# Moving the copies of keys and queries into block rows from the middle of a down stage to behind its output stores (mLSTM cell followed by a GELU layer)

## The chip, the cores and the metric

The kernel runs on one core of a Trainium2 chip. The metric is the device time of one execution in microseconds. A profile of one further execution gives the span from its first to its last instruction and what each engine did: TensorE (PE, with its weight loads PEld), VectorE (DVE), ScalarE (ACT), GpSimd (POOL) and SyncE (SP), which here does nothing but issue DMA transfers, one after the other.

## The reference

Two layers, one behind the other. The first is a recurrent cell over 4 batches, 8 heads, 768 steps and a head size of 40; its result, reshaped to 3072 rows of 320, goes through a feed-forward layer of width 2048 with an exact GELU.

```python
for t in range(S):
    m_new = np.maximum(f_gate[:, :, t] + m, i_gate[:, :, t])
    f_stab = np.exp(f_gate[:, :, t] + m - m_new)
    i_stab = np.exp(i_gate[:, :, t] - m_new)
    m = m_new
    C = f_stab[..., None, None] * C + i_stab[..., None, None] * einsum('bhd,bhe->bhde', vt, kt)
    n = f_stab[..., None] * n + i_stab[..., None] * kt
    y[:, :, t] = sigmoid(o_gate[:, :, t]) * einsum('bhde,bhe->bhd', C, qt) / max(|n.qt|, 1)
x = y.transpose(0, 2, 1, 3).reshape(3072, 320)
out = gelu_exact(x @ w_in) @ w_out
```

## The kernel before

The 768 steps are cut into six chunks of 128 (`c` = 0 to 5). For each chunk and each of the four batches `b` the cell is computed in its parallel form: masked decay weights `W` (loaded from `M_d`, masked on POOL, exponentiated on ACT), scores from `kT` and `qT`, values, and an update of the carried `state`. The 512 rows of a chunk then go through the feed-forward layer: an **up stage** (`up`, line 926: products with `w_in`, GELU into `g`) and a **down stage** (`down_steps`, line 1052: products of `g` with `w_out` into `po`, added up in `o_sb` and stored to `out`). PE runs them in turn: up of chunk 1, down of chunk 1, up of chunk 2, and so on. The cell of chunk `c + 1` is woven into the two stages of chunk `c`. The order within a down stage is written out by hand in the string `DOWN` (line 36), which `play` (line 1115) follows letter by letter: `F` is the next of 14 steps of down products, `M`, `W`, `G`, `S`, `C`, `V`, `Y`, `X`, `R` and others are steps of the cell, and `j` is `load_next`. Every engine executes its instructions in the order in which they were written.

From chunk 2 on, keys and queries are not transposed on PE. They are first copied from their input arrays into a scratch array in device memory, `kq_d`, in an order of block rows (`copy_chunk`, line 156: for each batch two DMAs of keys and two of queries, 80 KB each, 16 in all for a chunk). Later `load_blocks` (line 164, four DMAs) reads one batch of them into the tile `blocks` (or `blocks3` for the last batch), and DVE transposes that tile in 32 by 32 squares into `kT` and `qT` (`turn_k`, `turn_q`).

All these transfers stand in one queue, SP's, in the order written. In the built program each DMA of that queue also waits, ahead of being issued, for the one eight places before it to have landed. Around the change the queue holds, for a stage `c`:

- in the down stage: the block rows of batch 3 (`load_last`), the decay weights of batch 3 into a part of `g` (`last_M`), keys and values of batch 3; then at `j` the block rows of batch 0 of chunk `c + 2`, followed by `copy_chunk(c + 3)`;
- at the end of the down stage: the stores of `o_sb`. The twelfth `F` ends the product whose follow-up is `p3` (line 1099): a DVE addition into `o_sb[0]` and four stores (`send`, line 1025, two for each of two batches). The fourteenth and last `F` ends the one with `p4` (line 1104), likewise with four stores. The letters behind `j` are `R0 Y2 Y3 X1 F F X2 R1 F R2 X3 R3 F`;
- in the up stage of chunk `c + 1`: behind the transposes of batch 0 the block rows of batch 1 (`turn_q`), then the `later_loads` (line 979): weights `W`, keys `kb`, values `vb` and gates `ob` of the next cell, and behind the transposes of batch 1 the block rows of batch 2.

`copy_chunk` is called in four places of the kernel: for part of chunk 2 in the first part of the program, for the rest of chunk 2 and for chunk 3 in the up stage of chunk 1, and in `load_next` for chunk 4 (down stage of chunk 1) and chunk 5 (down stage of chunk 2). In the down stages of chunks 3 and 4 nothing is left to copy. A copied chunk is first read at `j` of the following down stage.

Of the kernel before, what the change touches and what calls it, by code (L numbers as in the profile page):

```python
# [41 lines left out]
def kernel(  # L42
# [18 lines left out]
    B, H, S, D = q.shape  # L61
    L = P
    NCH = S // L
# [92 lines left out]
    def copy_chunk(c, batches=range(B)):  # L156

        for b in batches:
            for i, src in enumerate((k, q)):
                for hip in range(2):  # L160
                    nc.sync.dma_start(out=kq_d[c - 2][b, hip].rearrange("(m i x t) d -> i x m (t d)", m=NP, i=2, x=16)[i],
                                      in_=src[b, hip::2, c * L:(c + 1) * L, :].rearrange("m (x t) d -> x m (t d)", x=16))

    def load_blocks(n, to):

        c, b = divmod(n, B)
        for hip in range(2):
            for d, w in ((0, 32), (32, D - 32)):
                nc.sync.dma_start(out=to[64 * hip + d:64 * hip + d + 32].rearrange("t m i (g w) -> t (m i g) w", w=32)[:, :, 0:w],
                                  in_=kq_d[c - 2][b, hip, :, d:d + w].rearrange("(x t) d -> t x d", t=32))  # L170
# [254 lines left out]
    class Cell:  # L425
# [73 lines left out]
        def load_next(self):  # L499
            if self.c + 1 < NCH:  # L500
                load_blocks((self.c + 1) * B, by_block)
            if self.c + 2 < NCH:
                copy_chunk(self.c + 2)

        def weigh_last(self, b):
            if self.c < NCH - 1:
# [518 lines left out]
    def send(c, b, o_sb):  # L1025
        to = out[b * S + c * L:b * S + (c + 1) * L, :]
        if c == 0:
            nc.sync.dma_start(out=to, in_=o_sb)
            return
        for a in range(2):  # L1030
            queue = nc.scalar if a and c == NCH - 1 else nc.sync
            queue.dma_start(out=to[halves[a]], in_=o_sb[a::2])
# [19 lines left out]
    def down_steps(c, g):  # L1052
        A = lambda e, h: lambda j, t: g.t[:, HF * e + j, HT * h + t * L:HT * h + (t + 1) * L]
        Sm = lambda s: lambda j, t: s[j // (HF // 2)][:, j % (HF // 2), t * L:(t + 1) * L]
        bank, o_sb = {}, {}

        def product(lhs, rhs, k, first, t, then):

            if first and t == 0:
                bank[k] = ps_mm.tile([P, 2, HD], F32, name="po", tag="b")  # L1060
            for j in range(HF):

                nc.tensor.matmul(bank[k][:, t, :], lhs(j, t), rhs(j), start=(first and t == 0 and j == 0),  # L1063
                                 stop=(t == 1 and j == HF - 1), skip_group_check=True)
            if t == 1:
                then(bank[k])

        def block(h, n):
            if h not in o_sb:
                o_sb[h] = outp.tile([P, 2, DM], F32, name="o_sb", tag="o_sb")  # L1070
            return o_sb[h][:, :, HD * n:HD * (n + 1)]

        def add(to, pb, x):
            nc.vector.tensor_tensor(out=to, in0=pb, in1=x, op=OP.add)


        def p1(pb):
            nc.scalar.copy(out=block(1, 1), in_=pb)

        def p6(pb):  # L1080
            add(block(1, 0), pb, block(1, 1))

        def p2(pb):
            nc.scalar.copy(out=block(0, 0), in_=pb)

        def sum_late():
            for i in range(2):
                a12 = g.t[:, HF + HF // 2 * i:HF + HF // 2 * (i + 1), 0:HT]
                nc.vector.tensor_tensor(out=a12, in0=a12, in1=g.s2[i], op=OP.subtract)

        def p5(pb):
            add(block(1, 1), pb, block(1, 0))

        def p7(pb):
            add(block(1, 1), pb, block(1, 1))
            if c == NCH - 2:
                nc.sync.dma_start(out=w_out[:, 0:HF, HD:], in_=right_d)

        def p3(pb):
            add(block(0, 1), pb, block(1, 0))  # L1100
            for t in range(2):
                send(c, t, o_sb[0][:, t, :])

        def p4(pb):
            add(block(1, 0), pb, block(1, 0))
            for t in range(2):
                send(c, 2 + t, o_sb[1][:, t, :])

        todo = ((A(0, 0), Bm[0][0], 0, True, p1), (Sm(g.s2), T[2], 1, True, p6),
                (A(1, 0), Bm[1][0], 0, False, p2), (Sm(g.s1), T[1], 2, True, p5),  # L1110
                (A(0, 1), T[3], 3, True, p7), (A(1, 0), Bm[1][1], 2, False, p3),
                (A(1, 1), T[4], 3, False, p4))
        return [lambda x=x, t=t: product(*x[0:4], t, x[4]) for x in todo for t in range(2)], sum_late

# [36 lines left out]
    for c in range(1, NCH):  # L1151
        if c + 1 == NCH:
            down = LastDown()
            up(None, [], [], down)
            down.products()
            break
        g, later = Hidden(True), []
        steps = cell_steps(c + 1, "MWGTscVYXRLKQDCBSjh", g)
        up(g, weight_sum(1) + weight_sum(2) + weight_sum(3) if c == 1 else [], [lambda b=b: (steps["K"](b), steps["Q"](b)) for b in range(2)])
        if c == 1:  # L1160
            later = weight_sum(4)
        products, late = down_steps(c, g)
        steps |= dict(F=in_turn(products), Z=in_turn(later), N=late)
        play(DOWN, steps)
# [30 lines left out]
```

## Time and profile before

| what | us |
|---|---|
| median of three runs | 462.73 (462.39 to 462.76) |
| the profiled execution | 462.86 |
| its span, first to last instruction | 460.7 |
| down stage of chunk 1 on PE | 153.82 to 198.35 |
| up stage of chunk 2 | 198.35 to 224.85 |
| down stage of chunk 2 | 224.85 to 268.09 |
| up stage of chunk 3 | 268.09 to 294.59 |
| down stage of chunk 3 | 294.59 to 337.29 |
| issue of the 16 copies of chunk 4 on SP | 174.54 to 188.02 |
| issue of the 16 copies of chunk 5 on SP | 245.14 to 257.98 |
| one copy from issue to landing, median | 2.5 |
| one store of `o_sb` from issue to landing, median | 2.0 |

The stages are read off the chain of work that ended last, where the first products of a stage (`pu` at line 947 for up, `po` at line 1063 for down) begin. A time on SP is the time that the issue of a DMA takes on that queue; the transfer itself runs on 16 DMA engines that all queues of the core share, and lands later. "Idle before" names what an engine waited for; "issue" there means a gap for which the profile shows no releaser.

### The profile page before, as it was taken

What the parts mean: (1) busy time and instruction counts of PE and PEld (TensorE: products, weight loads), DVE (VectorE), ACT (ScalarE), POOL (GpSimd) and SP (SyncE); (2) the same over time, 40 slices, a digit from 0 to 9 for tenths busy, and PEclk for the clock granted to TensorE, in tenths of its full rate; (3) what the DMA queues carried; (4) which work ended last, traced back from release to release, by engine and by line L of the source; (5) the groups of instructions that cost most, each with busy time, mean ns of one, the idle gap of its engine ahead of it and who ended that gap; (6) DMA issues with size and microseconds to landing.
All of it is one profiled execution on the core that took longest, in us unless ns stands there. A gap on an engine that the chain in (4) does not pass through costs nothing.

```text
span 460.7 us, 13113 instructions
## 1 busy us (share of the span) xinstructions
PE 451.9 (98%) x5432; PEld 402.0 (87%) x5432; DVE 308.7 (67%) x661; ACT 243.7 (53%) x541; POOL 76.7 (17%) x117
## 2 busy tenths in 40 slices
PE   9999999999999998999999999999999999999996
PEld 8787888877788898998899998899998899988996
DVE  8677457573579987755578754578654577699950
ACT  7886999953244593113494113395113395257701
POOL 3001030000010432200542200542300422100000
PEclk9999999999999999999999999999999999999999
DMA  7999962295857655219945219853018950200001
GB/s 168 221 221 223 232 177 69 82 242 125 166 129 158 113 96 98 57 51 182 167 79 103 59 57 184 154 92 46 3 57 168 172 94 15 80 35 1 1 0 58
DMA packets 174875, 51.12 MB, mean 111 GB/s; under 512 B 154752, under 2 KB 168352, under 8 KB 174816
## 3 DMA queue, kind: packets, MB, share of 16 engines
q1 hardware_dynamic: 174496, 49.95, 51.0%
q8 instruction: 43, 0.70, 0.6%
q10 hardware_dynamic: 320, 0.33, 0.2%
q14 instruction: 16, 0.13, 0.1%
HBM read 45.47 MB, written 10.03 MB: 120 GB/s over the span
## 4 chain that ended last, share of the span: by engine, by line
PE 95%; DVE 2%; issue 1%; DMA 1%; ACT 1%; SPq 0%; DVEq 0%
PE po L1063 26%; PE pu L947 23%; PE po L1042 8%; PE pu L804 6%; PE pu L958 6%; PE po L917 6%; PE ph L655 4%; PE ps L553 3%; PE pu L810 2%; PE ps L537 2%; PE px L695 2%; PE pf L608 2%; PE pt L515 1%; PE cold L226 1%; PE pf L619 1%; PE pf L575 1%
## 5 line engine op out<-in xcount | busy, mean ns | idle before, releaser
L1063 PE MATMUL po<-w_out,g 128*128 128x160 f32 x512 | 74.4, 302 | 0.0
L962 ACT ACTIVATE g<-pu 128x512 f32<-128x512 f32 x64 | 32.2, 618 | 77.4 <-PE pu L958 77.4
L1063 PEld LDWEIGHTS po<-w_out,g 128*128 128x128 f32 x512 | 70.1, 190 | 1.9 <-ACT g L962 1.3
L947 PE MATMUL pu<-x_hi,w_in_hi 128*128 128x512 f32 x160 | 39.0, 387 | 0.0
L465 ACT ACTIVATE W<-W,aT 128x128 f32<-128x128 f32 x128 | 38.7, 387 | 0.1
L947 PE MATMUL pu<-x_lo,w_in_lo 128*128 128x512 f32 x160 | 37.8, 379 | 0.0
L1063 PE MATMUL po<-w_sums,sums 128*128 128x160 f32 x256 | 36.9, 302 | 0.0
L439 POOL TENSOR_SCALAR_AFFINE_SELECT W<-W 128x1024 f32<-128x1024 f32 (+2 forms) x20 | 24.1, 1209 | 75.8 <-DMA W<-M_d 66.8
L1063 PEld LDWEIGHTS po<-w_sums,sums 128*128 128x128 f32 x256 | 35.0, 190 | 0.4
L1042 PE MATMUL po<-w_out,g 128*128 128x320 f32 x128 | 35.2, 433 | 0.0
L947 PEld LDWEIGHTS pu<-x_hi,w_in_hi 128*128 128x128 f32 x160 | 29.5, 189 | 5.7 <-ACT g L962 1.3
L947 PEld LDWEIGHTS pu<-x_lo,w_in_lo 128*128 128x128 f32 x160 | 30.2, 189 | 4.3
L1042 PEld LDWEIGHTS po<-w_out,g 128*128 128x128 f32 x128 | 24.0, 190 | 9.6
L524 POOL TENSOR_TENSOR vw<-vb,ewT 128x328 f32<-128x328 f32 x12 | 8.7, 737 | 138.5 <-DMA vb<-in_v_dram 55.9
L947 PE MATMUL pu<-x_all,w_mid 128*128 128x512 f32 x80 | 30.3, 379 | 0.0
L947 PE MATMUL pu<-x_all,w_in_mid 128*128 128x512 f32 x80 | 30.3, 379 | 0.0
L559 DVE TENSOR_TENSOR W<-ps,W 128x256 f32<-128x256 f32 (+1 forms) x48 | 18.1, 416 | 17.0 <-PE ps L553 7.1
L804 PE MATMUL pu<-first_x,w_in 128*128 128x256 f32 x128 | 28.8, 381 | 0.0
L804 PEld LDWEIGHTS pu<-first_x,w_in 128*128 128x128 f32 x128 | 23.8, 190 | 3.1
L791 DVE TENSOR_TENSOR sums<-g 128x512 f32<-128x512 f32 x16 | 12.3, 770 | 19.6 <-ACT g L962 19.6
L763 DVE TENSOR_TENSOR w_in_mid<-w_in_hi,w_in_lo 128x512 fp32r<-128x512 f32 x20 | 13.7, 686 | 16.5 <-PE pu L947 16.5
L385 DVE SCALAR_TENSOR_TENSOR pow<-sig,pow 128x320 uint32<-128x320 uint32 (+1 forms) x26 | 14.6, 563 | 13.7 <-ACT pow L375 13.7
(195 smaller groups left out, 917.5 us busy)
## 6 DMA issues: line engine op xcount, KB each, us to landing
W<-M_d SPq DMA_DIRECT2D x16, 512.0 KB, 5.4
bits<-in_moe_w_in_dram SPq DMA_DIRECT2D x20, 256.0 KB, 4.5
bits<-in_moe_w_out_dram SPq DMA_DIRECT2D x16, 320.0 KB, 3.2
blocks<-kq_d SPq DMA_DIRECT2D x32, 128.0 KB, 3.6
ob<-in_o_gate_dram SPq DMA_DIRECT2D x24, 160.0 KB, 3.9
out_dram<-o_sb SPq DMA_DIRECT2D x36, 80.0 KB, 2.0
kq_d<-in_k_dram SPq DMA_DIRECT2D x32, 80.0 KB, 2.5
kq_d<-in_q_dram SPq DMA_DIRECT2D x32, 80.0 KB, 2.5
```

The source lines that it names most:

```text
L385: nc.vector.scalar_tensor_tensor(out=p, in0=s, scalar=3, in1=p, op0=OP.logical_shift_left, op1=OP.bitwise_or)
L439: nc.gpsimd.affine_select(out=x, in_=x, compare_op=OP.is_ge, fill=1.0e30, base=base, pattern=[[0, H], [1, x.shape[2]]], channel_multiplier=-1)
L465: nc.scalar.activation(out=W[n][:, h, :], in_=src, func=AF.Exp, scale=-1.0, bias=aT[:, self.c, r:r + 1])
L559: nc.vector.tensor_tensor(out=w[r, :, t], in0=ps[i][hip][r, :, t], in1=w[r, :, t], op=OP.mult)
L655: nc.tensor.matmul(ph[r, h, :], Pm[:, h, r], vb[turn_of(n)][:, h, :], start=True, stop=True)
L804: nc.tensor.matmul(banks[-1][e][:, i - i0, :], in_tile(i, x)[:, e, i % 2 * P:(i % 2 + 1) * P], first_x[:, x, t0:t1], start=(x == 0 and i = ...
L917: nc.tensor.matmul(in_pairs(po[t]), x[:, t * L:(t + 1) * L], in_turns(w), start=(f, k) == first, stop=(f, k) == last, skip_group_check=True)
L947: nc.tensor.matmul(in_pairs(pus[i][e]), w[k][:, e, i * P:(i + 1) * P], in_turns(x[:, k, :]), start=(n == 0 and k == 0), stop=False, skip_g ...
L958: nc.tensor.matmul(in_pairs(pu[e]), w[r, i // 2, i % 2 * P:(i % 2 + 1) * P], in_turns(x[r, NX, :]), start=False, stop=(n == 2), skip_group ...
L962: nc.scalar.activation(out=g.t[:, HF * e + i, :], in_=pu[e], func=AF.Gelu, scale=4097.0)
L1042: nc.tensor.matmul(po[b], g.t[:, f, b * L:(b + 1) * L], w_out[:, f, :], start=(f == 0), stop=(f == NF - 1))
L1063: nc.tensor.matmul(bank[k][:, t, :], lhs(j, t), rhs(j), start=(first and t == 0 and j == 0), stop=(t == 1 and j == HF - 1), skip_group_che ...
```

## The change

`load_next` no longer calls `copy_chunk`. The 16 copies of chunk `c + 3` are issued by the down stage's own follow-ups instead: those of batches 0 and 1 behind the four stores of `p3`, those of batches 2 and 3 behind the four stores of `p4`. `c` in `load_next` is the chunk of the cell, one more than the chunk of the down stage, so the same chunks 4 and 5 are copied in the down stages of chunks 1 and 2.

```diff
         def load_next(self):
             if self.c + 1 < NCH:
                 load_blocks((self.c + 1) * B, by_block)
-            if self.c + 2 < NCH:
-                copy_chunk(self.c + 2)
@@
             for t in range(2):
                 send(c, t, o_sb[0][:, t, :])
+            if c + 3 < NCH:
+                copy_chunk(c + 3, range(2))
 
         def p4(pb):
             add(block(1, 0), pb, block(1, 0))
             for t in range(2):
                 send(c, 2 + t, o_sb[1][:, t, :])
+            if c + 3 < NCH:
+                copy_chunk(c + 3, range(2, B))
```

On PE, DVE, ACT and POOL the built program has the same instructions with the same waits in the same order; only the order on SP differs, in two places.

## The prediction

> **What bounds the kernel now.** I read the page first, then the time by stage, then SP's queue, then PE's waits.
>
> ```profile
> PE 451.9 (98%) x5432; PEld 402.0 (87%) x5432; DVE 308.7 (67%) x661; ACT 243.7 (53%) x541; POOL 76.7 (17%) x117
> ...
> 153.82:198.35 44.53, 42.87 (x813) 41.28 (x814) 35.84 (x84) 23.79 (x60) 14.89 (x22) 1.00 0.47 88
> 224.85:268.09 43.24, 42.86 (x813) 41.29 (x814) 31.60 (x68) 23.79 (x60) 15.04 (x22) 1.00 0.47 86
> 294.59:337.29 42.70, 42.65 (x813) 41.17 (x814) 30.70 (x68) 23.77 (x60) 16.30 (x21) 1.00 0.37 59
> ```
>
> PE is busy 451.9 of 460.7 us at full granted clock (the 1.00). The lower lines are the down stages of chunks 1, 2 and 3: length, then busy time of PE, PEld, DVE, ACT, POOL. PE is idle in them for 1.66, 0.38 and 0.05 us. All three run the same PE instructions, and only the first two hold copies. So the most a removal of the copies from the middle can bring is small, and the change loses only if PE starts to wait for a transfer.
>
> ```profile
> 193.94 7.36 SPq L1032 DMA_DIRECT2D out_dram<-o_sb  x8
> 206.10 2.29 SPq L169 DMA_DIRECT2D blocks<-kq_d  x4
> ...
> 223.58 6.76 SPq L169 DMA_DIRECT2D blocks<-kq_d  x8
> 231.46 0.38 SPq L186 DMA_DIRECT2D g<-M_d  x1
> 236.82 1.29 SPq L151 DMA_DIRECT2D kb<-in_k_dram  x2
> ...
> 248.66 1.23 SPq L161 DMA_DIRECT2D kq_d<-in_k_dram  x2
> 249.93 1.23 SPq L161 DMA_DIRECT2D kq_d<-in_q_dram  x2
> ```
>
> This is SP's timeline (start, length, what) from the end of the down stage of chunk 1 on. Single rows of it give the stores as 193.94 to 196.42 (`p3`) and 198.91 to 201.30 (`p4`, whose DVE addition starts at 198.39). Then SP waits 4.80 us for the DVE transpose of batch 0, which ends at 206.08. From 206.10 to 230.34 it issues one load after another. The `g` load waits for DVE's sums until 231.46, and the `kb` load for PE until 236.82.
>
> ```profile
> PE pf L619 <- issue: 1.1, 1, 1.1
> PE ph L655 <- issue: 0.3, 1, 0.3
> ```
>
> These are PE's own waits without a releaser: the first at 175.92 to 177.03 in the down stage of chunk 1, the second at 253.26 to 253.59 in that of chunk 2 (0.42 by the weight loads). Both lie where copies are in flight.
>
> **Part 1: what leaves the middle.** Sixteen issues go from SP in each of two stages (174.54 to 188.02, 245.14 to 257.98). The next on SP are the stores, which wait for DVE until 193.94 and 263.68, 5.9 and 5.7 us after the last copy, so the queue gains nothing there. What may gain is PE's instruction supply. The DMA queue marked "instruction" moved 43 packets, 0.70 MB, 16 KB each; that is 256 instructions of 64 B if all are PE's, and 43 x 256 = 11,008 fits PE's 10,864 matmuls and weight loads. In windows of a tenth of a microsecond, such a packet starts at 174.6 (1.10 us long by its share of the 16 engines) and at 251.2 (0.96 us). PE resumes 2.43 and 2.39 us after those starts. I therefore take both gaps as waits for instructions, in bursts of very short matmuls. How much of them the copies cause:
> - Chunk 1: at 174.6 the engines were over 90% busy with the block loads issued from 171.33, which stay; the first copy was only issued at 174.54. Bounds 0 and 1.11 us; I take 0, the row of the block loads being nearer.
> - Chunk 2: the packet itself took 0.96 us, as did those at 317.0 and 323.2 in chunk 3 with no copies (0.97, 0.96), and the wait behind it fell where the engines were idle (252.4 to 253.1). Only the time ahead of the packet can have been lengthened. Bounds 0 and 0.54 us, the whole difference to the stage of chunk 3 (43.24 - 42.70); I take 0.2, about half of the 0.42 gap.
>
> [...]
>
> **Part 2: what the end of the stage takes on.** In the quiet stretch 248.66 to 251.20 four copies took 2.54 us, 0.635 each. Behind the stores of `p3`: 8 x 0.635 = 5.08, 196.46 to 201.54. The stores of `p4`, ready at about 198.9, are pushed to 201.54 to 204.0 (2.6 us later). Nothing needs them soon: their tile is next written by ACT at 229.43. Then eight copies to 209.1. None waits long for the eighth before it, which was issued 5 us earlier and lands in 2.5. So the block rows of batch 1 are issued 3.0 us later (209.1 for 206.10), and the loads behind them, which stood without a gap, likewise. What each is needed for (landing: longest of `blocks` 5.5, median of `g` 4.8):
> - `blocks`, batch 1: landed by 216.9; DVE transposes it at 220.06 as its program order has it.
> - `vb`: POOL waited for it until 221.07, now 224.1. Behind it come a mask of W, a clearing of the block tile that started at 224.75, and the mask of the second W, which ended at 229.45 and will by about 230.7 (the clearing starts some 1.2 later). ACT reaches that W after eight exponentials from 231.17, at 233.6.
> - `blocks`, batches 2 and 3: landed by 238.8; DVE needs them at 240.24.
> - `g`: issued at about 233.8 and landed by 238.6; POOL masks it at 239.30.
> - `kb`: SP is free again at about 234, and it waits for PE until 236.82 anyway.
>
> So the lateness ends there, in SP's own waits. Chunk 1 shows the same lateness already: copies of chunk 3 stood in the queue before its down stage, and its `g` load is issued at 161.69 to 163.41, 9.6 us into the stage, against 7.0 in chunk 2.
>
> ```profile
> 161.69 1.72 SPq L186 DMA_DIRECT2D g<-M_d  x1
> ...
> 168.28 1.81 POOL L439 TENSOR_SCALAR_AFFINE_SELECT g<-g 64x1024 f32<-64x1024 f32 x2
> ...
> 239.30 1.81 POOL L439 TENSOR_SCALAR_AFFINE_SELECT g<-g 64x1024 f32<-64x1024 f32 x2
> ```
>
> The mask came 14.46 us into that stage (168.28 - 153.82) and 14.45 into chunk 2's, so 2.6 us of lateness cost nothing. Cost of this part: 0. If the cover were gone, each further microsecond would cost up to one per stage, twice. Instruction packets at the new place (213 and 231) feed an up stage of 146 matmuls in 26.5 us, where a late packet stalls nothing.
>
> **Sum.** -0.2 + 0 = -0.2 us: 462.66 for the profiled execution, which is 460.7 of span and 2.16 around it. It stands 0.13 above the median, so 462.5 for the median.
>
> **Rivals.**
> 1. Both gaps are the copies' doing and vanish: -(1.11 + 0.54) = -1.65, 461.1. For it: both lie beside copies and the stage without copies has none. Against it: the block loads at 174.6; besides, where the supply runs short depends on where a block of 256 instructions ends in a burst, and that differs from stage to stage.
> 2. The lateness outgrows its cover. In the middle of chunk 1 the first four copies took 174.54 to 178.20, 0.91 each. SP has 2.49 (between the stores) and 4.80 us idle to take them up, so the shift is 16 x 0.91 - 7.3 = 7.3 us. The cover of `g`: SP was done at 230.34 and may be done by 234.4 (239.30 less 4.8, less the issue) for no delay, 4.1; ACT's wait behind the mask (241.11 to 241.75) gives 0.6; and POOL's result of 247.54, which DVE takes at 248.52, 1.0: 5.7 in all. Beyond that PE's transposes of `y` come late: 2 x (7.3 - 5.7) = +3.2, 465.9. It decides from a shift of 5.7 us, 0.81 a copy. For it: the average of the 16 in the middle was 0.80 (12.84 / 16). Against it: those pauses came while block loads kept the engines busy, and at 196 to 206 only the stores run.
> 3. The copies run where they are put and no term above exists: 462.73. It differs from the forecast by less than can be told.
>
> **How the numbers follow.** A difference of 0.2% (0.93 us) is about what a measurement of this kernel can tell from no change. The forecast and rival 3 hold 0.54; rival 1, 0.22; rival 2, 0.24, higher than its rows alone would give, since the chain of loads behind the copies is long and one tight consumer that I passed over suffices. Rivals 1 and 2 lie beyond 0.2%, so faster 0.22, same 0.54, slower 0.24. The range starts at rival 1, less 0.1, and reaches to 464.4, a shift of 6.6 us (+1.7), which leaves out the further part of rival 2 and a little below.
>
> **What would show it.** SP's timeline: the block rows of batch 1 at about 209 and 279 instead of 206.10 and 275.85, the mask of `g` still 14.45 us into the stages of chunks 2 and 3. The down stage of chunk 1 still 44.5 with its gap at 177, that of chunk 2 at 43.0. The forecast is wrong if PE waits for `ps`, `pf` or `px` in the down stages of chunks 2 or 3, or if the gap of chunk 1 is gone.

## The result and the profile after

The changed kernel ran at a median of 463.68 us over 20 runs (462.70 to 465.90), the kernel before beside it at 462.44 (20 runs, 461.85 to 463.56): a ratio of 1.0026 with a 95% interval of 1.0016 to 1.0036. It was slower, by little. The profiled execution was one of the shortest of the 20 (462.74, span 460.6), so its total says nothing of the loss; its stages show where PE lost time. Four later comparisons of the same two kernels, on four chips, gave 1.000 to 1.0013 (experiments 1, 5, 10 and 14), so the loss is not the same everywhere.

The down stages of chunks 1, 2 and 3 after the change (window, length, then busy time of PE, PEld, DVE, ACT, POOL, granted clock, DMA share, GB/s):

```profile
153.57:197.82 44.25, 42.87 (x813) 41.28 (x814) 35.77 (x84) 23.79 (x60) 15.86 (x22) 1.00 0.36 60
224.32:267.47 43.15, 42.87 (x813) 41.29 (x814) 31.73 (x68) 23.81 (x60) 15.01 (x23) 1.00 0.44 72
293.96:337.15 43.19, 42.94 (x814) 41.34 (x814) 31.80 (x68) 23.90 (x60) 16.95 (x23) 1.00 0.46 78
```

Chunk 1 is 0.28 us shorter and chunk 2 0.09, but chunk 3, in whose down stage nothing was ever copied, is 0.49 longer (42.70 before; a second profile of the kernel before, experiment 9, has 43.43, 43.16 and 42.98, so one profile tells differences of this size only roughly). That stage comes right after the up stage whose loads now stand behind the copies of chunk 5. SP's timeline there (start, length, what):

```profile
265.56 1.29 SPq L161 DMA_DIRECT2D kq_d<-in_k_dram  x2
266.89 2.59 SPq L161 DMA_DIRECT2D kq_d<-in_q_dram  x2
...
272.14 2.46 SPq L1030 DMA_DIRECT2D out_dram<-o_sb  x4
...
279.82 2.92 SPq L169 DMA_DIRECT2D blocks<-kq_d  x4
...
297.61 7.27 SPq L169 DMA_DIRECT2D blocks<-kq_d  x8
305.05 0.58 SPq L186 DMA_DIRECT2D g<-M_d  x1
305.94 1.60 SPq L151 DMA_DIRECT2D kb<-in_k_dram  x2
```

The block rows of batch 1 start 12.35 us into the up stage (279.82 - 267.47; 7.76 before, so 4.6 late), and the `g` load 11.1 us into the down stage (305.05 - 293.96) instead of 6.6. In the up stage of chunk 2 the delay is 3.3 (208.84 - 197.82 = 11.02 for 7.75). POOL now waits for `g` (the bracket is the idle time before and its releaser):

```profile
239.39 1.81 POOL L439 TENSOR_SCALAR_AFFINE_SELECT g<-g 64x1024 f32<-64x1024 f32 x2 [0.57 <-DMA g<-M_d]
...
309.84 1.80 POOL L439 TENSOR_SCALAR_AFFINE_SELECT g<-g 64x1024 f32<-64x1024 f32 x2 [1.37 <-DMA g<-M_d]
```

The mask comes 15.07 and 15.88 us into the two stages, for 14.45. PE's own waits, however, still name no engine beyond those of before:

```profile
PE pf L617 <- issue: 0.8, 1, 0.8
...
PE ph L653 <- issue: 0.2, 1, 0.2
PE pf L606 <- issue: 0.2, 1, 0.2
```

The first is still that of chunk 1 (1.1 before), without a copy in that stage's middle. The last is new, and lies in chunk 3.

### The profile page after: what moved, and what is told of

Read it like the earlier page. It is cut to its first block, busy times and chain, and to the rows that moved or that the text cites. A ratio compares the mean times of both kernels' runs of the same rounds, so it can differ in the third digit from the quotient of the medians.

```text
span 460.6 us, 13113 instructions
## 1 busy us (share of the span) xinstructions
PE 452.0 (98%) x5432; PEld 401.5 (87%) x5432; DVE 310.8 (67%) x661; ACT 243.7 (53%) x541; POOL 76.5 (17%) x117
## 4 chain that ended last, share of the span: by engine, by line
PE 92%; DVE 4%; ACT 1%; DMA 1%; issue 1%; SPq 0%; DVEq 0%
PE po L1061 26%; PE pu L945 23%; PE po L1040 8%; PE pu L956 6%; PE po L915 6%; PE pu L802 5%; PE ph L653 4%; PE ps L551 3%; PE ps L535 2%; PE pf L606 2%; PE px L693 2%; PE pu L808 2%; PE pt L513 1%; PE pf L617 1%; PE pf L573 1%
## 5 line engine op out<-in xcount | busy, mean ns | idle before, releaser
L557 DVE TENSOR_TENSOR W<-ps,W 128x256 f32<-128x256 f32 (+1 forms) x48 | 18.1, 416 | 16.7 <-PE ps L551 7.1
L703 ACT ACTIVATE x_hi<-px 128x384 fp32r<-128x384 f32 x20 | 9.7, 486 | 25.6 <-PE px L693 25.6
```

The lines of the kernel that those rows point to most:

```text
L557: nc.vector.tensor_tensor(out=w[r, :, t], in0=ps[i][hip][r, :, t], in1=w[r, :, t], op=OP.mult)
```

## The experiments

Four theories were told apart. Q: SP's loads are pushed back behind the copies. T: the copies' traffic at the border of the stages does it, whatever the queue. Q was later split into M (the late mask of `g` holds up ACT, VectorE and PE) and S (the late `g` load shares the DMA engines with PE's packets of instructions, and PE runs dry). Each had up to 12 timed runs beside the kernel before; diffs are against the changed kernel. "Stages" are the lengths of the down stages of chunks 1, 2 and 3 in the profile, good to about 0.01 us.

**1. The changed kernel again** (no edit).

> The changed kernel itself once more, for a second profile and more times: about 1.0026 of before. Theory Q (the queue): the loads of the up stage stand behind 16 copies on SP and start 3 to 4.5 us later, and the decay weights of batch 3 (g) come too late for POOL, ACT and then PE; a profile of a typical execution (463.2 and more) shows the down stage of chunk 3, chunk 2 or both 0.5 to 1.5 us longer than before (42.70 and 43.24), with POOL waiting for the DMA of g by 0.6 to 3 us. Theory T (the traffic): the copies slow something at the border of the stages by sharing the DMA engines there; then the up stages of chunks 2 and 3 (26.50) or the last products of the down stages before them are longer, and POOL's wait for g does not go with the loss.

Measured: 1.000 (0.9987 to 1.0013). Stages 43.70, 43.15, 42.71. Here `g` is issued 10.2 us into the stage of chunk 3, and that stage loses nothing. The loss is not there in every execution, and this profile shows none of it.

**2. Half of the copies behind p3, half at j.**

```diff
             if self.c + 1 < NCH:
                 load_blocks((self.c + 1) * B, by_block)
+            if self.c + 2 < NCH:
+                copy_chunk(self.c + 2, range(2, B))
...
-            if c + 3 < NCH:
-                copy_chunk(c + 3, range(2, B))
```

> Batches 0 and 1 are copied behind the stores of p3, batches 2 and 3 at j as before. Eight copies take 5.1 us of SP, and it has 2.5 and 4.8 us idle there: the block rows of batch 1 start at most 0.3 us later. Theory Q: 1.000 of before (0.999 to 1.0005), and g masked 14.45 us into the stages of chunks 2 and 3. Theory T: half of the traffic is at the border, so about half of the loss, 1.0013.

Measured: 0.9992 (0.9982 to 1.0002), stages 43.44, 43.15, 43.01. Block rows of batch 1 at 7.75 us, `g` at 6.61, mask at 14.45, all as before. So eight copies do fit into SP's idle time, as theory Q has it. The time does not part Q from T, since the changed kernel itself was at 1.000 on that chip.

**3. The copies behind p4 issued by ACT.**

```diff
-    def copy_chunk(c, batches=range(B)):
+    def copy_chunk(c, batches=range(B), queue=nc.sync):
...
-                copy_chunk(c + 3, range(2, B))
+                copy_chunk(c + 3, range(2, B), nc.scalar)
```

> As the changed kernel, but the eight copies behind the stores of p4 are issued by ACT, which is idle there for 11 us until the GELUs. The same traffic at the same place, but SP's loads are not pushed. Theory Q: the loss is gone, 0.9985 to 1.0003 of before, block rows of batch 1 within 0.5 us of the place they have before. Theory T: the loss stays, about 1.0026.

Measured: 0.999 (0.998 to 1.000), stages 43.20, 42.88, 42.72. SP's loads are where they were, and every stage is among the shortest seen. All 16 copies are still at the border of the stages, but not quite where the changed kernel has them: ACT issues its eight from 2.1 us before the up stage to 3 or 4 us into it, while SP in the changed kernel issues them 6 to 12 us into it. So this run speaks against T without settling it. What settles it are the up stages, in which the copies now run: T expects them longer, and those of chunks 2 and 3 take 26.49 or 26.50 us in every profile, of before and after alike.

**4. Only the copies of chunk 5 moved.**

```diff
+            if self.c + 2 < NCH - 1:
+                copy_chunk(self.c + 2)
...
-            if c + 3 < NCH:
+            if c + 3 == NCH - 1:
                 copy_chunk(c + 3, range(2))
...
-            if c + 3 < NCH:
+            if c + 3 == NCH - 1:
                 copy_chunk(c + 3, range(2, B))
```

> Only the copies of chunk 5 (end of the down stage of chunk 2) are moved; those of chunk 4 stay at j. Theory Q: the loads of the up stage of chunk 3 are the later ones (the first profile showed the g load 4.5 us later into that stage, 2.5 in chunk 2), so most of the loss is here: 1.0015 to 1.003, with the down stage of chunk 3 at 43.2 or more and that of chunk 2 as before or up to 0.5 shorter. Theory T: half, 1.0013, shared evenly with the copies of chunk 4.

Measured: 1.0001 (0.9991 to 1.0012), which misses the expected time, but stages 43.57, 42.88, 43.85: chunk 3 has lost 1.15 us, chunk 2 nothing. PE's gap there (0.77 us) again has no releaser, though ACT had waited 0.9 for POOL's late mask. That is where M and S part in chunk 3.

**5 and 6. The changed kernel and the ACT variant on a second chip.**

> The changed kernel a third time, beside the others of this job on one chip. So far it was 1.0026 of before in one place and 1.000 in another. Theory S (the supply): SP's shift of 3.3 us in chunk 2 and 3.9 to 4.6 in chunk 3 moves the 512 KB of the g load from 6.6 to 9 to 11 us into the down stage, onto PE's packet of instructions that was fetched 13.9 us into it; PE runs dry in the burst of short matmuls behind (0.2 to 0.8 us). What the copies cost in the middle (0.3 to 1 us over two stages) and what they cost at the end nearly cancel: 0.999 to 1.003, and the instruction packet of the down stage of chunk 3 starts at 14.8 us or later. Theory M (the mask): the loss comes over the late mask of g, ACT's exponentials and VectorE, so the longer stage shows PE waiting for an engine, not for nothing.

> The variant with the copies behind p4 issued by ACT, once more. Theories S and M, which both go by SP's queue: faster than the changed kernel of this job by 0.1 to 0.3%, 0.998 to 1.000 of before, g issued 6.6 us into the down stages of chunks 2 and 3. Theory T (the traffic at the border): the same as the changed kernel.

Measured: 1.0005 (0.9991 to 1.0019) and 0.9994 (0.9981 to 1.0007). Stages 43.85, 42.85, 44.09 and 43.18, 42.86, 42.69. The profile of the changed kernel shows the loss at its plainest. SP's timeline and PE's, chunk 3, whose down stage begins at 292.97:

```profile
304.29 0.44 SPq L186 DMA_DIRECT2D g<-M_d  x1
304.94 1.32 SPq L151 DMA_DIRECT2D kb<-in_k_dram  x2
```

```profile
313.24 1.03 PE L606 MATMUL pf<-state,qT 64*64 64x41 f32 x55
315.29 0.31 PE L606 MATMUL pf<-state,qT 64*64 64x41 f32 x3 [1.02 <-issue]
```

PE stops for 1.02 us inside one line's burst of 64 short matmuls, and the profile shows no releaser ("issue"). In the view of the DMA queues, in windows of a tenth of a microsecond, the packets of 16 KB for PE start at 15.6 and 20.0 us into this stage, where the kernel before has 13.9 and 17.4. PE goes on 2.3 us after the second (315.29 - 313.0). The DMA share (next to last column) shows what the first packet meets. Changed kernel, from 12 to 15 us into the stage:

```profile
304.97:305.97 1.00, 1.00 (x19) 0.95 (x14) 0.95 (x3) 0.99 (x3) 0.98 (x2) 1.00 0.80 108
305.97:306.97 1.00, 1.00 (x9) 1.00 (x9) 0.99 (x5) 0.99 (x2) 1.00 (x2) 1.00 1.17 230
306.97:307.97 1.00, 1.00 (x52) 0.83 (x54) 0.99 (x4) 0.99 (x3) 0.50 (x1) 1.00 0.87 236
```

Kernel before, from 12 to 15 us into the same stage:

```profile
306.59:307.59 1.00, 1.00 (x20) 0.95 (x14) 0.95 (x3) 0.99 (x3) 0.97 (x2) 1.00 0.00 0
307.59:308.59 1.00, 1.00 (x9) 1.00 (x9) 0.99 (x5) 0.99 (x2) 1.00 (x2) 1.00 0.53 94
308.59:309.59 1.00, 1.00 (x52) 0.83 (x54) 0.99 (x4) 0.99 (x3) 1.00 (x2) 1.00 0.48 71
```

Before, `g` has landed by 11.7 us and the engines show a share of 0.00 until 13, then of 0.53 and 0.48 with keys; after, `g` and keys show 0.80 to 1.17, and `g` lands at 16.0. Such a share alone does not push the packet: in experiment 1 it is 0.82 and 1.03 from 12 to 14 us, and the packet still starts at 13.9. There `g` lands at 14.5. In which order the DMA engines serve the two is not shown.

**7. g alone late.** Eight copies straight ahead of the `g` load, none behind p4.

```diff
         def last_M(self, b):
+            if self.c + 2 < NCH:
+                copy_chunk(self.c + 2, range(2, B))
             load_M(self.c * B + b, self.before.t[:, 0:HF, P:2 * P])
...
-            if c + 3 < NCH:
-                copy_chunk(c + 3, range(2, B))
```

> Eight copies behind the stores of p3, which pushes nothing, and the other eight straight ahead of the g load, so that in the down stages of chunks 1 and 2 g alone is late, at about 10.6 us, while the loads of the up stage stay where they are before. Theory S: both stages lengthen by 0.3 to 1 us over those of the variant with half behind p3 (43.44 and 43.15) by gaps of PE without a releaser, 1.0005 to 1.003 of before. Theory M: as long or longer, but PE waits for VectorE (ps, px). If neither g nor its place matters (the loss being that of vb, W and the block rows): 0.999 to 1.000, stages as in that variant.

Measured: 1.0044 (1.0027 to 1.0061), more than expected, since `g` came later than planned (13.3 and 11.9 us). Stages 44.99, 43.58, 42.69, with PE gaps of 1.15 and 0.66 us without a releaser. The loads of the up stage are where they were, so a late `g`, with eight copies just ahead of it, is enough. ACT waited up to 3.1 us for the masks, yet PE for no engine that it had not waited for before.

That is not yet S in both stages. In chunk 1 a packet starts 17.2 us into the stage, beside a `g` load that lands at 18.2; the kernel before has it at 15.6 (and a gap of about the same length, 1.11). In chunk 2 `g` lands at 16.7, and the packet ahead of the gap starts only at 251.5, 26.9 us into the stage, when the engines are empty:

```profile
250.00:251.00 1.00, 1.00 (x10) 1.00 (x9) 0.99 (x4) 0.69 (x3) 0.43 (x3) 1.00 0.00 0
251.00:252.00 1.00, 1.00 (x53) 0.83 (x55) 0.97 (x5) 0.00 (x0) 0.78 (x2) 1.00 0.06 16
```

What is late there is VectorE's last product for `ob`, which PE transposes into `px`. It ends 25.3 us into the stage with the late mask (first line) and 24.5 in the kernel before (second line):

```profile
249.14 0.74 DVE L677 TENSOR_TENSOR ob<-ob,den 128x320 f32<-128x320 f32 x1 [0.57 <-POOL ob L672]
...
248.86 0.49 DVE L677 TENSOR_TENSOR ob<-ob,den 128x320 f32<-128x320 f32 x1
```

In all sixteen profiles this packet starts 1.5 to 1.9 us behind the end of that product, which lies between 24.5 and 29.2 us into the stage, and a block of 256 PE instructions (see below) begins just at these transposes. That suggests, and does not show, that the packet is asked for only when PE's sequencer gets past them. By this reading the late mask (M) acts here through the supply of instructions, with a DMA share of 0.00 to 0.06 around the packet and so without sharing the engines: M and S do not exclude each other.

**8. A small g load.**

```diff
-            nc.sync.dma_start(out=to, in_=src.unsqueeze(0).to_broadcast([P, H, L]))
+            nc.sync.dma_start(out=to[:, 0:1], in_=src[0:1].unsqueeze(0).to_broadcast([P, 1, L]))
```

> As the changed kernel, but the g load brings one head of eight (64 KB for 512 KB); the other seven heads of batch 3 keep what stood there, so they compute something else in the same time. The loads of the up stage are as late as in the changed kernel. Theories S and M: no collision and no late mask, so the down stages of chunks 2 and 3 are 42.7 to 42.9 and the total 0.997 to 0.9995. If it is the lateness of the other loads: as the changed kernel, 43.0 to 43.9 in chunk 3.

Measured: stages 43.42, 42.85, 42.69, with `g` issued at 10.9 us in chunk 3 and block rows as late as in the changed kernel. By the stages the loss is gone, with all 16 copies in the changed kernel's place; but so it is in three of the five profiles of the changed kernel, so one profile is weak evidence. The first packet of chunk 3 still starts 0.7 us late (14.6), which costs nothing. The time is 1.0005 (0.9991 to 1.0019) and misses the expectation; the first part of the program, which no edit touches, took 126.7 to 128.8 us in these profiles (128.1 here, 126.8 in run 5), and hides differences of this size.

**9 to 12. Before against itself, the changed kernel, four copies more, four copies fewer,** all on a third chip.

> The kernel before against itself: 1.000 within the interval, which shows what such a comparison can tell. Its profile is a second one of the stages: theory S has the 1.11 us gap of PE in the down stage of chunk 1 and the 0.33 us in chunk 2 come from packets of instructions that had to share the engines with block loads and copies, so they may differ by some tenths between executions: 43.5 to 44.8 and 42.9 to 43.4; chunk 3, with nothing beside the packets, stays 42.7.

Measured: 0.9995 (0.9981 to 1.0009), stages 43.43, 43.16, 42.98. Chunk 1's gap of 1.1 us is absent here, with all 16 copies in its middle. Chunk 3 misses the 42.7 that was expected: with `g` early and the first packet on time it is 0.28 us longer than in the first profile, since its second packet starts 1.4 us later (table below). So up to 0.3 us of that stage comes and goes without a late `g`.

> The changed kernel a fourth time. Theory S: 1.000 to 1.0026 of before; the down stage of chunk 3 is 42.7 where its instruction packet keeps its place at 13.9 us and 43.2 to 44.2 where it is pushed to 14.8 us or later by the g load, with a gap of PE 2.3 us behind a packet.

Measured: 1.0005 (0.9986 to 1.0025). Stages 43.42, 42.89, 42.71, `g` at 10.1 in chunk 3. Its twelve times fall into 460.9 to 461.5 (five) and 462.8 to 465.7 (seven). The profiled one, 463.05, is of the upper group, yet PE has no gap in its three stages; its first part took 128.8 us. So the two groups are not shown to be the packets' doing.

```diff
             if c + 3 < NCH:
                 copy_chunk(c + 3, range(2, B))
+                copy_chunk(c + 3, range(2, 3))
```

> As the changed kernel with four copies more behind the stores of p4 (batch 2 a second time, the same bytes to the same place), so that SP's loads start another 2.5 us later: block rows of batch 1 at 13.6 us into the up stage of chunk 2, g at 11.8 us into its down stage and at 13 or later in chunk 3. Theory S: both stages lose by gaps of PE, and g is now also masked beyond its cover (over 16.5 us into the stage): 43.3 or more in chunk 2, 43.5 or more in chunk 3, 1.002 to 1.006 of before. If lateness were not the cause (theory T, traffic): a quarter more traffic, no more than a quarter more loss than the changed kernel beside it.

Measured: 1.0116 (1.0084 to 1.0147), nearly twice the upper end expected. The `g` load starts at 238.57, 14.3 us into the stage of chunk 2, 7.6 later than before. PE's gaps in that stage:

```profile
253.89 0.44 PE L693 MATMUL px<-ident,ob 128*128 128x128 f32 x2 [2.19 <-DVE ob L675]
257.37 0.27 PE L653 MATMUL ph<-vb,g 128*32 128x41 f32 x5 [1.48 <-issue]
```

Now PE waits in both ways: 2.19 us for the chain from the mask over ACT to VectorE (M), and 1.48 for instructions. The second is no collision: the DMA share is 0.00 from 250 to 254, and the packet starts at 255.0, 1.6 us behind the product that ended the first wait, as in experiment 7. From its first product to that of the next stage, chunk 2 takes 47.4 us, for 43.0 in the kernel before, and chunk 3 43.2 for 42.5; together that is about the loss of the medians (467.16 for 462.19). In chunk 3, where `g` is issued only at 12.7 us, PE's added wait is for VectorE (0.5 us, `ps`), the packets start at 14.3 and 18.1, and PE has no gap without a releaser. A quarter more traffic did many times the harm, so it is not the traffic as such.

```diff
+            if self.c + 2 < NCH:
+                copy_chunk(self.c + 2, range(3, B))
...
-                copy_chunk(c + 3, range(2, B))
+                copy_chunk(c + 3, range(2, 3))
```

> Batches 0 and 1 behind the stores of p3, batch 2 behind those of p4, batch 3 at j: 12 copies of 7.6 us for the 7.3 us that SP has idle. Theory S: the loads are 0.3 to 0.8 us later, g at most 7.4 us into the stage, chunk 3 at 42.7, and 0.998 to 1.0003 of before, under the changed kernel beside it. Theory T: three quarters of the changed kernel's loss.

Measured: **0.9984 (0.9973 to 0.9994)**, the only variant whose interval lies wholly below 1, on one chip with twelve runs. Stages 43.19, 43.20, 42.70. SP in the down stage of chunk 3, which begins at 294.00:

```profile
295.31 6.43 SPq L169 DMA_DIRECT2D blocks<-kq_d  x8
301.91 1.28 SPq L186 DMA_DIRECT2D g<-M_d  x1
```

`g` starts 7.9 us into the stage, 0.5 later than expected, and has landed (12.8) before the packet of 13.9 is due. The block rows of batch 1 were 0.7 and 1.5 us late, more than planned.

**13 and 14. g ahead of the block rows of batch 3,** and the changed kernel beside it on a fourth chip. All 16 copies stay at the end.

```diff
 DOWN = """
-    M0 F Z F L3 W0 M1 Z W1 S0 C0 F F h0 Q2 F K2 G1 D3 B3 Z V0 ...
+    M0 F Z F B3 L3 W0 M1 Z W1 S0 C0 F F h0 Q2 F K2 G1 D3 Z V0 ...
```

> As the changed kernel, with the same 16 copies at the same place, but the g load of every stage is issued ahead of the block rows of batch 3 instead of behind them (it waits there for VectorE's sums at 6.4 us into the stage, and those block rows come behind it). Loads of the up stage stay as late as in the changed kernel; only g is early again. Theory S: no packet of instructions is pushed, the down stage of chunk 3 is 42.7 to 42.9 in every profile and the times lose their upper group: 0.997 to 0.9995 of before, 0.1 to 0.3% under the changed kernel beside it. If the block rows, now the last of the chain, collide with the packet in the place of g, or if the lateness of W and vb counts: as the changed kernel.

> The changed kernel beside the one with g ahead, on the same chip: 1.000 to 1.0026 of before. Theory S: its times fall into those near 461.5 and those of 462.5 and more, by whether g, issued 10.1 to 11.3 us into the down stage of chunk 3, comes before or after the request for the packet at 13.9.

Measured: 0.9999 (0.9988 to 1.0011) with `g` ahead, 1.0013 (1.0001 to 1.0025) without; medians 461.76 and 462.64. The first misses its expectation, the twelve times of the second form no two groups, and the intervals overlap, so the times alone do not part the two. With `g` ahead the stages are 43.45, 43.03, 42.95: nothing like 43.9, but not 42.7 either, for the block rows of batch 3 now end at 306.5, 12.9 us into the stage, and the packet starts at 14.9.

Put together, the length of the down stage of chunk 3 goes by where its packets start (us into the stage, by tenths; all profiles but that of twenty copies, where VectorE lengthens the stage):

| kernel | g issued | packets | stage |
|---|---|---|---|
| before | 6.6 | 13.9, 17.4 | 42.70 |
| changed, again | 10.2 | 13.9, 17.4 | 42.71 |
| changed, fourth chip | 10.3 | 14.1, 17.5 | 42.70 |
| g alone late (chunks 1 and 2) | 6.6 | 13.9, 17.5 | 42.69 |
| copies on ACT | 6.6 | 13.9, 17.6 | 42.72 |
| copies on ACT, second chip | 6.6 | 13.9, 17.6 | 42.69 |
| small g | 10.9 | 14.6, 18.1 | 42.69 |
| changed, third chip | 10.1 | 14.1, 18.5 | 42.71 |
| twelve at the end | 7.9 | 14.0, 18.5 | 42.70 |
| g ahead | 7.1 | 14.9, 18.8 | 42.95 |
| before, again | 6.6 | 14.0, 18.8 | 42.98 |
| half behind p3 | 6.6 | 14.0, 18.8 | 43.01 |
| changed, first profile | 11.1 | 14.8, 19.0 | 43.19 |
| only chunk 5 | 10.8 | 15.3, 19.7 | 43.85 |
| changed, second chip | 11.3 | 15.6, 20.0 | 44.09 |

Up to 18.5 for the second packet the stage is free of loss; behind that it grows with the packet, 1 us for about 1 us. A full `g` load issued by 10.3 leaves the first packet at 13.9 to 14.1; with one issued from 10.8 to 11.3 it starts at 14.8 to 15.6. In the rows at 42.95 to 43.01 `g` was early: there the first packet was late behind block rows (`g` ahead), or only the second was late, for a reason that the profiles do not show.

That these are waits for instructions can be seen by counting. Counted over all rows of PE and its weight loads in a trace, semaphore instructions included, PE has 23 waits of 0.1 us or more without a releaser behind the first part of the program, in twelve of the sixteen profiles. Each stands behind instruction 3,777, 4,033, 6,337 or 7,873: always 193 more than a multiple of 256. And 256 is about what a packet brings: 43 packets for the 10,959 instructions so counted are 254.9 each, and 43 x 16,384 bytes are 64.3 bytes for each instruction. Each ends 2.2 to 2.6 us after a packet starts. And in chunk 3 PE runs instructions 6,900 to 7,868 at the same times into the stage, within 0.05 us, in the fourteen profiles that can be compared one by one; the five long stages among them then lose 0.15, 0.18, 0.39, 1.01 and 1.24 us at instruction 7,873, most of what they are longer.

## Why the prediction was wrong

It forecast 462.5 and no change that can be told; measured was +0.26%. The time lay inside the range, the direction was not forecast.

- **What leaves the middle, chunk 2: -0.2.** Right in kind, small in size. With no copies in its middle that stage took 42.85 to 42.89 in six profiles, against 43.24 and 43.16 of the kernel before; in four others without them it was 43.03 to 43.19. Neither the issue of `g` (6.5 to 10.0 us in these four, 6.6 to 10.5 in the six) nor the start of the packet (26.0 to 26.3 and 26.0 to 26.1) parts the two groups; the difference falls on instruction 6,337, and why PE waits longer there in some of them is open.
- **Chunk 1: 0.** Right on average. Its gap was 1.1 us and absent in two profiles of the kernel before, and 0.8, 0.3, 0.3 and twice absent in five of the changed one. It comes and goes in either, so the copies in the middle are not its cause alone; that the block loads are was not tried.
- **SP's shift of 3.0 us.** 3.3 in chunk 2, as worked out. In chunk 3 it was 3.5 to 4.6: copies paused there (2.59 us for two at 266.89). The same shift had been taken for both.
- **The landing of g by 238.6 and its mask at 239.30.** Missed by a little: POOL waited 0.57 and 1.37 us in the first profile. ACT and VectorE covered it, as rival 2's sum of 5.7 us for the cover had it; with `g` 7.6 late (experiment 11) PE waited 2.19 for VectorE, where 7.6 - 5.7 gives 1.9.
- **"Cost of this part: 0" is the step that failed.** The prediction followed each late load to the engine that reads it and found cover at each. It did not ask what each late load, while it is under way, would meet on the DMA engines. It looked at instruction packets only where the copies went (213 and 231), and wrote that a late packet stalls nothing there. But the `g` load, moved from 6.6 to 10 or 11 us into the down stage, can meet the packet due at 13.9, ahead of a burst of short matmuls; in the five profiles of the changed kernel chunk 3 took 42.70, 42.71, 42.71, 43.19 and 44.09 us, so that cost 0 to 1.4 us where 0 was put.
- **Chunk 1 as a witness misled.** Its `g` load is issued 7.9 us into the stage, not 11, and has landed at 13.1, ahead of the packet that starts at 15.6. The 2.6 us are the difference of the ends of the two issues; by their starts it is 1.3 (7.87 for 6.61).
- **Rival 2** had the right place (`g`), sign and cause (a shift larger than its cover), but not the way to PE: its chain over ACT and VectorE made PE wait openly only with twenty copies, and otherwise, in chunk 2 of experiment 7, as it seems by making the request for instructions late (packet 26.9 us into the stage, for 26.4 before). Rival 1 fell: neither gap was the copies' alone.
- **Both gaps as waits for instructions.** That reading held (the counting above). The supply runs only a little ahead of PE here: a packet 2.6 us late (20.0 for 17.4) went with a stage 1.4 longer, and in no profile does a packet start while PE has more than 300 instructions left before the block that it brings, counted as above (297 at most in the first profile of the kernel before, 296 in that of the changed one).

What stays open is how much of the measured loss this step makes up. The first comparison gave 1.0026, 1.24 us, with 17 of 20 times at 463.2 or more; the four later ones gave 1.000, 1.0005, 1.0005 and 1.0013. The three stages together take 130.5 and 129.6 us in the two profiles of the kernel before, and 129.0 to 130.8 in the five of the changed one, on average 130.0 and 129.8, so the profiles do not account for 1.24 us, and none shows one of those 17 executions. The granted clock is not the reason: the twelve of the 20 at 1.000 have a median of 463.4. That the distance between `g` and a packet differs from chip to chip would fit, and is not shown. No total of one run parts theories here, only stages do.

## What to carry to other kernels

When transfers are moved in a queue, list two things for everything behind them: when its reader needs it, and what else is on the DMA engines when it will now run, instruction packets included (here three of them started 0.9 to 1.7 us later beside a late `g`, in stages 0.5 to 1.4 us longer). Fill an idle stretch of a queue to its length and no further: 12 copies in 7.3 us of idle gained 0.16% (on one chip), 16 gained nothing or lost up to 0.26%, 20 lost 1.2%. Where one run varies by as much as the effect, compare stages that an edit touches and not totals.

## What the runs showed of the hardware

PE's instructions come in packets of 16 KB: the DMA queue marked "instruction" moved 43 of them, 0.70 MB, 0.6% of the time of the same 16 DMA engines that carry the data (kernel before, view of the DMA queues), for PE's 10,959 instructions. PE resumed 2.2 to 2.6 us after the start of such a packet (23 gaps). In a burst that runs 64 matmuls in 0.80 us (`ph`, line 655, at 322.26 in the kernel before) PE stopped for 0.33 us at 253.26, so it can use up what is loaded before the next is there. The gaps stand whole multiples of 256 PE instructions apart. A gap of PE that the profile puts down to nothing ("issue") in such a burst could be traced here by the start of the packet ahead of it. That packet was late beside a `g` load still under way (14.8 to 15.6 us into the stage for 13.9, chunk 3 of the changed kernel on two chips and of experiment 4), or behind a wait of PE for another engine (2.19 us in chunk 2 with twenty copies; the packet started 1.6 us behind the product that ended it, at a DMA share of 0.00).
